# Seven block products instead of eight in rounds of the second channel layer, where attention stands still

## The chip, the cores and the metric

The kernel runs on one core of a Trainium2 chip. The metric is device time in microseconds (us) for one execution. A core has five engines with instruction queues of their own: TensorE (PE, matmuls; its weight loads are listed as PEld), VectorE (DVE), ScalarE (ACT), GpSimd (POOL) and SyncE (SP, which issues DMAs). A matmul writes to PSUM, from where DVE or ACT move or add the result to SBUF. Engines wait for one another through semaphores.

## The reference

Attention with a block mask is followed by a Fourier mixing block. Cut to what matters:

```python
# q, k, v: (4 batches, 8 heads, 768 tokens, 64), float32
scores = scale * np.matmul(q, k.transpose(0, 1, 3, 2))      # masked by blocks of 32
attn = softmax(scores)                                      # written out in full
x = heads_side_by_side(np.matmul(attn, v))                  # (4, 768, 512)

X = np.fft.fft(np.fft.fft(x, axis=1), axis=2)
u = x + np.real(X)
un = (u - mean(u)) / np.sqrt(var(u) + 1e-06)
ch = np.maximum(un @ w_ch1, 0.0) @ w_ch2                    # 512 -> 2048 -> 512
return u + ch
```

The last line but one holds the two channel layers. The change is in the second, `... @ w_ch2`.

## The kernel before, in words

**Order of the work.** The program is written out in full by a Python planner. Attention runs over 4 batches x 4 pairs of heads, in slots: a slot has the scores (L577, `s`), the exponential (L597), the mask multiply (L607) and the products with the values (L651, `o`); sums of the weights are made by POOL (L637). The Fourier and channel work of a batch is done while attention works on later batches. For that it is put into two lists: `apart`, small steps of the Fourier part (transforms `zp`, `pq`, statistics, whitening `un`, transposes `utp`, sums for the next products), and `late`, the channel steps. A model of the engines, `busy(engine, us)`, keeps a clock for PE, ACT, DVE and POOL, and `gap(...)` puts those steps of `apart` into the stream whose inputs and PSUM bank are free by that model. `until(met)` empties `late` until a condition holds. It is called where the attention of batch b needs the buffer x of batch b-2, and at the very end. While it runs, attention stands still: no new scores are issued.

**Halves.** The 768 tokens of a batch are folded into two halves of 384, with sums in xA and xB (tiles of 128 x 3 x 512). A half has three token groups m of 128.

**Rounds.** The 2048 hidden columns are done in rounds r = 0..3 of 512. A round begins with two quads (`quad(p)`), each of which makes two of the round's four hidden blocks of 128 for both halves, by a scheme with seven products for a 2 x 2 block product (L1066, tiles `xp`, `yp`, `z5`, `z7`), and leaves hA and hB after the relu. Then comes the second layer. In batches 0 to 2, `channels(r, half, m)` runs six times: four matmuls of 128x512 (`y`, L1122) into a PSUM tile of its pool, and one DVE sum `x += y` (L1125). In the records of the profile an fp32 matmul shows as two. In the last batch, `outputs(r, m, after)` does two rounds at once with seven block products of 128x256 (`yy`, L1187), whose PSUM tiles come from four different pools (`ps_m`, `ps_t`, `ps_s`, `ps_o`); its DVE sums are L1194 and L1217, an ACT copy L1204, and its left-hand sums L1170.

**Names that matter below.** `right` (L1028) makes the first layer's right-hand sums on DVE. L760 and L802 scale x and fold the Fourier parts, L886 to L903 are the matmuls of `pq`, L936 and L925 belong to statistics and `x += un`, L950 whitens, L991 transposes `un` (24 matmuls for a batch, `utp`), and L992 copies the result. `place` (L674, `xt`) writes the attention output into x. `store(half, m)` sends a finished token group to the output on SP's queue.

In the seven-product scheme, for blocks a of the hidden values (by half and by the first or second 256 of the round's hidden columns) and blocks B of the weights, sums of blocks are multiplied and the results are shared between output blocks, so that seven products of 128x256 do the work of eight.

Of the kernel before, what the change touches and what calls it, by code (L numbers as in the profile page):

```python
# [11 lines left out]
FP32 = mybir.dt.float32  # L12
# [5 lines left out]
ALU = mybir.AluOpType  # L18
ACT = mybir.ActivationFunctionType
# [80 lines left out]
def kernel(  # L100
# [14 lines left out]
    nc = tc.nc  # L115

    B, H, S, D = q.shape
    DM = H * D
    FF = w_ch1.shape[1]
    P = 128  # L120
# [56 lines left out]
    ep = ctx.enter_context(tc.tile_pool(name="ep", bufs=4))  # L177
    acc_p = ctx.enter_context(tc.tile_pool(name="acc_p", bufs=2))
    sum_p = ctx.enter_context(tc.tile_pool(name="sum_p", bufs=1))
    big = ctx.enter_context(tc.tile_pool(name="big", bufs=1))  # L180
    tr_p = ctx.enter_context(tc.tile_pool(name="tr_p", bufs=2))
    zc_p = ctx.enter_context(tc.tile_pool(name="zc_p", bufs=1))
# [12 lines left out]
    def busy(engine, us, after=0.0):  # L195
        when[engine] = max(when[engine], after) + us
        return when[engine]

    def bank(tag):

        at = free[tag].index(min(free[tag]))
        when["PE"] = max(when["PE"], free[tag][at])
        free[tag][at] = float("inf")
        return tag, at
# [6 lines left out]
    def room(i, shape, name, dtype=FP32):  # L211
        return big.tile(shape, dtype, tag=f"big{i}", name=name)
# [764 lines left out]
    def mixer(b, xA, xB):  # L977
# [75 lines left out]
        def quad(p):  # L1053

            g = p // 2 % 2 if last else 0
            if p % 2 == 0:
                for i in range(2):
                    hs[g, i] = room((2, 0)[g] + i, [P, 4, HS], "h" + "AB"[i])
            l1, l2 = 2 * (p % 2), 2 * (p % 2) + 1
            h11, h12, h21, h22 = (hs[g, i][:, l, :] for l in (l1, l2) for i in range(2))  # L1060
            a11, a12, s2, a22 = blocks(p)
            b11, b21, b22 = unT[0][:, K1, :], unT[0][:, K2, :], unT[1][:, K2, :]

            def product(to, a, c, after=0.0):
                for k in range(ND // 2):
                    nc.tensor.matmul(to, a[:, k, :], c[:, k, :], start=(k == 0),  # L1066
                                     stop=(k == ND // 2 - 1))
                return busy("PE", PRODUCT, after) + HOP

            def plus(to, ps, a, at):  # L1070
                tt(out=to, in0=ps, in1=a, op=ALU.add)  # L1071
                return busy("DVE", SUM, at) + HOP

            def relu(h, at):
                nc.scalar.activation(out=h, in_=h, func=ACT.Relu)  # L1075
                busy("ACT", RELU, at)

            def combine(j):
                left(p + 1, j)
                busy("DVE", COMBINE)  # L1080

            x, at = ps_m.tile([P, 512], FP32, tag="m", name="xp")[:, 0:HS], bank("m")
            z5, z7 = (ps_s.tile([P, 2, 512], FP32, tag="s", name=name)[:, 0, 0:HS]
                      for name in ("z5", "z7"))
            done = product(x, a11, b11)
            nc.scalar.copy(out=h11, in_=x)  # L1086
            p1 = busy("ACT", RELU, done) + HOP
            give(at, p1 - HOP)
            y, at = ps_m.tile([P, 512], FP32, tag="m", name="yp")[:, 0:HS], bank("m")
            p2 = product(y, a12, b21)  # L1090
            done = product(z7, s2, t[2])
            u2 = plus(h21, z7, h11, max(done, p1))
            c11 = plus(h11, y, h11, p2)
            relu(h11, c11)
            done = product(z5, s[1], t[1])
            plus(h12, z5, h21, done)
            combine(1)
            done = product(z7, s[3], t[3], u2)
            u3 = plus(h21, z7, h21, done)
            c22 = plus(h22, z5, h21, done)  # L1100
            z_at[0] = c22
            relu(h22, c22)
            combine(3)
            gap(0.0, 1.9)
            done = product(y, a22, t[4], c11)
            c21 = plus(h21, y, h21, done)
            give(at, c21 - HOP)
            relu(h21, c21)
            gap(0.0, 1.9, "t")
            done = product(z7, s[4], b22, u3)  # L1110
            z_at[1] = plus(h12, z7, h12, done)
            relu(h12, z_at[1])
            combine(4)
            if last:
                for j in ((1, 2), (3, 4))[p % 2]:
                    output_right(p // 4, j, p // 2 % 2)

        def channels(r, half, m):

            y, at = ps_m.tile([P, DM], FP32, tag="m", name="y"), bank("m")  # L1120
            for l in range(4):
                nc.tensor.matmul(y, hs[0, half][:, l, m * P:(m + 1) * P], w2_sb[:, 4 * r + l, :],  # L1122
                                 start=(l == 0), stop=(l == 3))
            x = (xA, xB)[half]
            nc.vector.tensor_tensor(out=x[:, m, :], in0=y, in1=x[:, m, :], op=ALU.add)  # L1125
            give(at, busy("DVE", 0.7, busy("PE", 3.45) + HOP))
            if r == NF // 4 - 1:
                store(half, m)

        def store(half, m, cols=slice(0, DM), queue=nc.sync):  # L1130
            x = (xA, xB)[half]
            for p0, cnt, rows in _rows(out[b][:, cols], T * half + m):
                queue.dma_start(out=rows, in_=x[p0:p0 + cnt, m, cols])
            if m == out_of[half][-1]:
                finished.add((b, half))

        last = b == B - 1  # L1140
        OUT = (2, 0, 1)
        out_of = (OUT, OUT if last else (0, 1, 2))
# [131 lines left out]
    short, apart, late, due = deque(), deque(), deque(), deque()  # L1274
    asked = set()
    needed = set()
    state = {"paired": False, "total": None, "w": 0, "got": 0, "owed": 0.0, "ready": 0.0}

    def channel_step():
        late.popleft()[0]()  # L1280
# [6 lines left out]
    def do_apart():  # L1287
        kind, fn, pe, act, dve, _ = apart.popleft()
        if kind[0] in "dw":
            dve += behind(kind)  # L1290
            state["ready"] = busy("DVE", dve, rstd_at[0] if kind == "w" else state["ready"]) + HOP
            fn()
            return
        done = state["ready"]
        if kind != "-":
            at = bank(kind[0])
            done = busy("PE", pe, done) + HOP
        fn()
        if act:
            done = busy("ACT", act, done) + HOP  # L1300
        if dve:
            done = busy("DVE", dve, done) + HOP
        if kind != "-":
            give(at, done - HOP)
        state["ready"] = done

    def gap(rest=0.0, ahead=None, kinds="tm"):

        used = "".join(k for k in "tm" if k not in kinds)
        if ahead is None:  # L1310
            ahead = AHEAD if late else ALONE
        while apart:
            kind, fn, pe, act, dve, need = apart[0]
            if len(late) > need:
                break
            if kind[0] in "dw":
                dve += behind(kind)
                if kind == "w" and rstd_at[0] > max(when["DVE"], when["PE"]) + 0.2:
                    break
                if max(when["DVE"], state["ready"]) + dve > when["PE"] + rest + ahead:  # L1320
                    break
            elif kind != "-":
                bank_at = max(min(free[k]) for k in kind)
                if (any(k in used for k in kind) or
                        max(state["ready"], bank_at) > when["PE"] + 0.1):
                    break
                used += kind
            do_apart()
        for item in list(short):
            kind, ready, fn = item  # L1330
            if kind not in used and max(ready, min(free[kind])) <= when["PE"] + 0.1:
                used += kind
                short.remove(item)
                fn()

    def until(met):

        while not met():
            if late:
                channel_step()  # L1340
                gap(2.0)
            else:
                do_apart()

    def begin(b):

# [16 lines left out]
    def once(*of):  # L1363
        if of in asked:
            return False
        asked.add(of)
        return True
# [11 lines left out]
    def slot(sl):  # L1379
# [46 lines left out]
        if s == 0 and 0 < n < len(pairs) - 1:  # L1426
            load_k(n + 1)

        reuse = n % NP == 0 and phase >= 2
        if s >= (5 if reuse else 3) and (n, 0) in oT_at and once(n):  # L1430
            b, j = pairs[n]
            at = oT_at[n, 0]
            if reuse:
                until(lambda: (b - 2, 0) in finished)
                at = when["PE"] + LEAVES
            if in_blocks(n):
                place_blocks(n, 0)
            else:
                short.append(("t", at, lambda: place(n, 0)))
# [97 lines left out]
        if sl == B * SB - 2:  # L1537
            over = nc.values_load(flag[0:1, 0:1], min_val=0, max_val=1)
    begin(B - 1)
    until(lambda: len(finished) == 2 * B)  # L1540
    ordered.close()


# [102 lines left out]
```

## Time and profile before

| What | Value |
|---|---|
| Median of 3 runs | 1062.39 us (1061.66 to 1063.84) |
| The profiled execution's own time | 1061.69 us |
| Span of that execution (first to last instruction) | 1060.0 us |
| Mean granted TensorE clock | 0.994 |
| DVE, ACT, POOL busy | 669.1, 366.5, 240.5 us |
| Matmuls of L1122 (`y`) | 576 records, 256.1 us busy |
| Matmuls of L1187 (`yy`), in the page's chain of waits | 7% of the span |
| Matmuls of L1122 in the chain of waits | 23% of the span |
| HBM traffic | 36.72 MB read, 6.29 MB written |

Durations in the page's groups are those of single instructions; for PE they overlap, so that the time a stream of matmuls takes is read from the starts of successive rows in the order in time. The last column of a group's row is the idle time of the engine just before its instructions, with the engine, tile and line that ended it. In a table by windows, the numbers after the window are its length and, for PE, PEld, DVE, ACT and POOL in turn, the busy time and count; then the granted clock (PEclk, 1.00 is full speed), the DMA share and GB/s. Rows of the order in time are: start, length, engine, line, operation, output and inputs, partitions and shape, count, and in brackets the idle time before and what ended it.

### The profile page before, as it was taken

The page shows a single profiled execution, that of the slowest core. Times are in us where ns is not written, and L with a number is a line of the kernel's source. Part 1 is how long each engine was busy: PE and PEld are TensorE (multiplying, and loading weights), DVE is VectorE, ACT ScalarE, POOL GpSimd, SP SyncE. Part 2 cuts the span into 40 slices and gives each one's busy share as a digit, 9 for nine tenths or more (in the row PEclk, how much of TensorE's full clock was granted, in tenths as well). Part 3 has the DMA queues.
Part 4 walks back from the last instruction along what each step waited for, and adds up shares of the span by engine and source line. Part 5 has one row for each costly group of instructions (what it writes and reads, how often), then busy time and mean ns, then how long its engine had stood idle before and what let it go on. Part 6 is the DMA issues. An engine that isn't in the chain of part 4 may idle for free.

```text
span 1060.0 us, 12495 instructions
## 1 busy us (share of the span) xinstructions
PE 1030.6 (97%) x4414; PEld 537.1 (51%) x4414; DVE 669.1 (63%) x1227; ACT 366.5 (35%) x736; POOL 240.5 (23%) x270
## 2 busy tenths in 40 slices
PE   8989999999999999999999999899999999999996
PEld 4333345445465454443534654354445564578585
DVE  6898795877746345655678364765447446774663
ACT  6978755564020122433441212343221111210210
POOL 1000183556000002554552001635420001000000
PEclk9999999999999999999999999999999999999998
DMA  7757522220000002231220001210000001000001
GB/s 217 229 166 222 112 46 45 45 46 15 1 1 0 1 1 57 52 56 27 41 54 0 1 1 44 63 33 19 8 15 0 1 0 42 19 1 1 0 18 46
DMA packets 120544, 46.27 MB, mean 44 GB/s; under 512 B 108172, under 2 KB 113562, under 8 KB 120474
## 3 DMA queue, kind: packets, MB, share of 16 engines
q1 hardware_dynamic: 119222, 44.66, 17.6%
q10 hardware_dynamic: 1220, 0.72, 0.3%
q8 instruction: 36, 0.59, 0.2%
q14 instruction: 34, 0.28, 0.1%
q0 software_dynamic: 32, 0.01, 0.0%
HBM read 36.72 MB, written 6.29 MB: 41 GB/s over the span
## 4 chain that ended last, share of the span: by engine, by line
PE 87%; DVE 6%; ACT 4%; issue 2%; DMA 1%; SPq 0%; POOL 0%; ACTq 0%; DVEq 0%; POOLq 0%
PE y L1122 23%; PE z L1066 16%; PE s L577 11%; PE o L651 10%; PE yp L1066 8%; PE yy L1187 7%; PE xp L1066 4%; PE zp L855 2%; PE s L587 1%; DVE t L1028 1%; ACT e L597 1%; PE sp L718 1%; PE sp L732 1%; PE utp L991 1%; PE xt L674 1%
## 5 line engine op out<-in xcount | busy, mean ns | idle before, releaser
L637 POOL TENSOR_TENSOR acc<-acc,e 128x384 f32<-128x384 f32 x158 | 160.9, 1052 | 87.1 <-DVE e L607 68.0
L577 PE MATMUL s<-qT,kT 64*128 64x384 f32 x768 | 154.8, 518 | 7.4 <-ACT e L597 5.8
L651 PE MATMUL o<-e,vr 128*64 128x384 f32 x768 | 143.1, 500 | 2.2 <-DVE oT L659 2.2
L1125 DVE TENSOR_TENSOR x<-y,x 128x512 f32<-128x512 f32 x72 | 49.8, 691 | 130.1 <-PE y L1122 129.8
L1122 PE MATMUL y<-w_sb,hB 128*128 128x512 f32 x288 | 128.0, 595 | 0.3 <-DVE x L1125 0.3
L1122 PE MATMUL y<-w_sb,hA 128*128 128x512 f32 x288 | 128.1, 594 | 0.0
L607 DVE TENSOR_TENSOR e<-s,mask 128x768 f32<-128x768 f32 x88 | 80.0, 950 | 48.9 <-ACT s L605 39.9
L577 PEld LDWEIGHTS s<-qT,kT 64*128 64x128 f32 x768 | 64.5, 187 | 85.7 <-ACT e L597 23.6
L605 ACT ACTIVATE s<-s 128x768 f32<-128x768 f32 x88 | 66.7, 792 | 92.6 <-PE s L577 92.4
L637 POOL TENSOR_TENSOR acc<-e 128x384 f32<-128x384 f32 x46 | 50.3, 1113 | 212.0 <-ACT e L597 125.9
L597 ACT ACTIVATE e<-s 128x768 f32<-128x768 f32 x104 | 79.1, 810 | 49.0 <-PE s L587 36.4
L1066 PE MATMUL z<-unT,t 128*128 128x384 f32 x256 | 93.4, 487 | 0.6 <-DVE hA L1071 0.6
L1122 PEld LDWEIGHTS y<-w_sb,hB 128*128 128x128 f32 x288 | 53.5, 190 | 65.5 <-issue 64.6
L1122 PEld LDWEIGHTS y<-w_sb,hA 128*128 128x128 f32 x288 | 53.6, 190 | 62.6 <-issue 59.9
L651 PEld LDWEIGHTS o<-e,vr 128*64 128x64 f32 x768 | 48.0, 136 | 72.7 <-issue 67.8
L1071 DVE TENSOR_TENSOR hA<-z,hA 128x384 f32<-128x384 f32 x64 | 35.7, 557 | 70.6 <-PE z L1066 70.6
L1075 ACT ACTIVATE hA<-hA 128x384 f32<-128x384 f32 x64 | 33.6, 524 | 122.5 <-DVE hA L1071 122.4
L1066 PEld LDWEIGHTS z<-unT,t 128*128 128x128 f32 x256 | 48.2, 190 | 35.6 <-DVE hA L1071 3.0
L1075 ACT ACTIVATE hB<-hB 128x384 f32<-128x384 f32 x64 | 33.6, 525 | 86.0 <-DVE hB L1071 86.0
L938 POOL TENSOR_SCALAR st<-st 128x1 f32<-128x1 f32 x24 | 8.3, 347 | 207.4 <-DVE st L937 207.3
L1086 ACT COPY hA<-xp 128x384 f32<-128x384 f32 x32 | 15.3, 479 | 111.6 <-PE xp L1066 111.6
L1066 PE MATMUL z<-t,w_sb 128*128 128x384 f32 x128 | 46.7, 488 | 0.7 <-DVE t L1028 0.7
(207 smaller groups left out, 1430.7 us busy)
## 6 DMA issues: line engine op xcount, KB each, us to landing
wraw<-in_moe_w_ch_dram SPq DMA_DIRECT2D x32, 512.0 KB
vr<-in_v_dram SPq DMA_DIRECT2D x30, 192.0 KB
qb<-in_q_dram SPq DMA_DIRECT2D x44, 96.0 KB
kb<-in_k_dram SPq DMA_DIRECT2D x44, 96.0 KB
x<-oT SPq DMA_DIRECT2D x192, 12.0 KB
out_dram<-x SPq DMA_DIRECT2D x11, 252.0 KB
out_dram<-x SPq DMA_DIRECT2D x18, 128.0 KB
qr<-in_q_dram SPq DMA_DIRECT2D x24, 64.0 KB
```

The lines of the kernel that those rows point to most:

```text
L577: nc.tensor.matmul(s[:, i, 0:HS], kT[rows, c * P:(c + 1) * P], qT[rows, queries], start=True, stop=u not in by_pe)
L597: nc.scalar.activation(out=e, in_=s[:, :, 0:HS], func=ACT.Exp, scale=scale)
L605: nc.scalar.activation(out=s[:, :, 0:HS], in_=s[:, :, 0:HS], func=ACT.Exp, scale=scale)
L607: nc.vector.tensor_tensor(out=e, in0=s[:, :, 0:HS], in1=m.broadcast_to([P, 2, HS]), op=ALU.mult)
L637: nc.gpsimd.tensor_add(out=acc[:, i, :], in0=start[:, i, :], in1=e[:, i, :])
L651: nc.tensor.matmul(o[D * i:D * i + D, :], vt[:, i, c, :], e[:, i, :], start=(c == 0), stop=(c == C - 1))
L1066: nc.tensor.matmul(to, a[:, k, :], c[:, k, :], start=(k == 0), stop=(k == ND // 2 - 1))
L1071: tt(out=to, in0=ps, in1=a, op=ALU.add)
L1075: nc.scalar.activation(out=h, in_=h, func=ACT.Relu)
L1122: nc.tensor.matmul(y, hs[0, half][:, l, m * P:(m + 1) * P], w2_sb[:, 4 * r + l, :], start=(l == 0), stop=(l == 3))
L1125: nc.vector.tensor_tensor(out=x[:, m, :], in0=y, in1=x[:, m, :], op=ALU.add)
L1187: nc.tensor.matmul(ps, a[:, k, :], c[k // 2][:, k % 2, :] if isinstance(c, list) else c[:, k, :], start=(k == 0), stop=(k == 3))
```

## The change

In batches 0 to 2, the quad that begins a round while `until(..., alone=True)` runs marks that round as one of seven products. That holds for eight of the twelve rounds: all four of batch 0, and the last two (r = 2, 3) of batches 1 and 2. In the second quad of such a round, outstanding sums of attention are drained, four buffers of the mask tiles' pool `ep` are taken as room, and POOL makes four right-hand sums of weight blocks (`round_right`). Then `round_of(r, m)` replaces the six `channels` steps by three, one for each token group, both halves together. Each has seven products of two matmuls of 128x256, all into the four quarters of one PSUM tile `ps` (two banks, pool `ps_s` with two buffers). The results are taken up by three ACT copies (`keep`), DVE sums straight from PSUM (`plus`, and one over both halves), and three POOL sums of what was kept (`later`). The left-hand sums of the next group are made by DVE (1, 2) and POOL (3, 4). Stretches of attention stand still one slot earlier than before where `late` is not empty (s = 4 instead of 5). The two halves of a batch now finish together. The core of the diff:

```diff
+            if not last:
+                if p % 2 == 0:
+                    seven[p // 2] = state["alone"]
+                elif seven[p // 2]:
+                    state["drain"]()
+                    sums_room()
+                    for j in (1, 2, 4, 3):
+                        round_right(p // 2, j)
...
+        def sums_room():
...
+            rooms = [ep.tile([P, 2 * HS], FP32, tag="e", name="of") for _ in range(4)]
+            w_t[1] = wt_p.tile([P, 2, DH], FP32, tag="wt", name="wt")
...
+        def round_right(r, j):
+            a, c = {1: (part(r, 0, 1), part(r, 0, 0)), 2: (part(r, 1, 1), w_t[1]),
+                    3: (part(r, 1, 1), part(r, 0, 1)), 4: (part(r, 1, 0), w_t[2])}[j]
+            nc.gpsimd.tensor_tensor(out=w_t[j], in0=a, in1=c, op=ALU.subtract)
+            busy("POOL", 1.35)
...
+        def round_left(m, j):
+            a11, a12, a21, a22 = tokens(m)
+            to, a, c, op = {1: (h_s[1], a21, a22, ALU.add), 2: (a21, h_s[1], a11, ALU.subtract),
+                            3: (h_s[3], a22, a21, ALU.subtract),
+                            4: (h_s[4], a12, a21, ALU.subtract)}[j]
...
+        def round_of(r, m):
...
+            ps = ps_s.tile([P, 2, 512], FP32, tag="s", name="yz")
+            u_at, c_at, d_at, o_at = ps[:, 0, 0:DH], ps[:, 0, DH:DM], ps[:, 1, 0:DH], ps[:, 1, DH:DM]
+
+            def product(to, a, c, start):
+                for k in range(2):
+                    nc.tensor.matmul(to, a[:, k, :], c[:, k, :], start=start and k == 0,
+                                     stop=k == 1, skip_group_check=True)
+                return busy("PE", 0.87) + HOP
...
+            done = product(u_at, a11, part(r, 0, 0), True)
+            k0 = keep(0, u_at, done)
+            done = product(c_at, a12, part(r, 1, 0), False)
+            k0 = max(k0, plus(a0, c_at, done))
+            later(a0, 0, k0)
+            gap(0.0, 1.9)
+            done = product(o_at, a22, w_t[4], True)
+            plus(b0, o_at, done)
+            if m == OUT[0]:
+                round_left(m, 3)
+                round_left(m, 4)
+            done = product(u_at, a21, w_t[2], False)
+            k1 = keep(1, u_at, done)
+            later(a1, 1, k1)
+            done = product(d_at, h_s[1], w_t[1], False)
+            k2 = keep(2, d_at, done)
+            ahead(1, 2)
+            gap(0.0, 1.9)
+            done = product(u_at, h_s[3], w_t[3], False)
+            tt(out=both, in0=both, in1=_at(ps[:, 0, :], 0, [(0, 2), (1, DH)]), op=ALU.add)
+            at = busy("DVE", 0.7, done) + HOP
+            later(b1, 2, max(at, k2))
+            ahead(3)
+            done = product(d_at, h_s[4], part(r, 1, 1), False)
+            plus(a1, d_at, done)
+            ahead(4)
+            gap(0.0, 1.9)
+            z_at[0] = z_at[1] = when["DVE"]
...
         def channels(r, half, m):
 
+            if seven.get(r):
+                round_of(r, m)
+                if m == OUT[-1]:
+                    for _ in range(T):
+                        late.popleft()
+                return
...
-    def until(met):
+    def until(met, alone=False):
+
+        state["alone"] = alone
...
+        def drain():
+            while due:
+                sum_up()
+        state["drain"] = drain
+
-        if s >= (5 if reuse else 3) and (n, 0) in oT_at and once(n):
+        if s >= ((4 if late else 5) if reuse else 3) and (n, 0) in oT_at and once(n):
...
-                until(lambda: (b - 2, 0) in finished)
+                until(lambda: (b - 2, 0) in finished, s == 4)
...
+    state["drain"] = lambda: None
+    until(lambda: len(finished) == 2 * B, True)
```

In the changed kernel's trace the seven products' matmuls stand on L1181.

More of the change, by code (lines that the diff above doesn't have):

```diff
@@ L179 @@
     sum_p = ctx.enter_context(tc.tile_pool(name="sum_p", bufs=1))
+    wt_p = ctx.enter_context(tc.tile_pool(name="wt_p", bufs=1))
     big = ctx.enter_context(tc.tile_pool(name="big", bufs=1))
@@ L1116, in quad, with cut @@
                     output_right(p // 4, j, p // 2 % 2)
-        def channels(r, half, m):
+        seven = {}
+        w_t, h_s, kept = {}, {}, {}
+        def sums_room():
+            def cut(t, at, k):
+                return t[:, at:at + 2 * HS // 3 * k].rearrange("p (k n) -> p k n", k=k)
+            rooms = [ep.tile([P, 2 * HS], FP32, tag="e", name="of") for _ in range(4)]
+            w_t[1] = wt_p.tile([P, 2, DH], FP32, tag="wt", name="wt")
+            for t, j in zip(rooms, (2, 3, 4)):
+                w_t[j] = t[:, 0:2 * DH].rearrange("p (k n) -> p k n", n=DH)
+            for t, j in zip(rooms, (1, 3, 4)):
+                h_s[j] = t[:, 2 * DH:2 * HS].rearrange("p (k n) -> p k n", n=P)
+            for i in range(3):
+                kept[i] = rooms[3][:, i * DH:(i + 1) * DH]
@@ new lines, in part, with tokens @@
+        def part(r, k, n):
+            return w2_sb[:, 4 * r + 2 * k:4 * r + 2 * k + 2, n * DH:n * DH + DH]
+        def round_right(r, j):
[3 more added lines that the diff above has]
+            busy("POOL", 1.35)
+        def tokens(m):
+            return [hs[0, i][:, 2 * k:2 * k + 2, m * P:(m + 1) * P]
+                    for i in range(2) for k in range(2)]
@@ new lines, in round_left @@
+        def round_left(m, j):
[3 more added lines that the diff above has]
+                            4: (h_s[4], a12, a21, ALU.subtract)}[j]
+            if j > 2:
+                nc.gpsimd.tensor_tensor(out=to, in0=a, in1=c, op=op)
+                busy("POOL", 0.75, when["DVE"])
+            else:
+                tt(out=to, in0=a, in1=c, op=op)
+                busy("DVE", 0.43)
@@ new lines, in round_of, with keep, plus, later @@
+        def round_of(r, m):
+            after = dict(zip(OUT, OUT[1:])).get(m)
+            a11, a12, a21, a22 = tokens(m)
+            a0, a1 = xA[:, m, 0:DH], xA[:, m, DH:DM]
+            b0, b1 = xB[:, m, 0:DH], xB[:, m, DH:DM]
+            both = xB[:, m, :].rearrange("p (n d) -> p n d", n=2)
+            ps = ps_s.tile([P, 2, 512], FP32, tag="s", name="yz")
[5 more added lines that the diff above has]
+                return busy("PE", 0.87) + HOP
+            def keep(i, src, done):
+                nc.scalar.copy(out=kept[i], in_=src)
+                return busy("ACT", 0.36, done) + HOP
+            def plus(to, src, done):
+                tt(out=to, in0=src, in1=to, op=ALU.add)
+                return busy("DVE", 0.43, done) + HOP
+            def later(to, i, at):
+                nc.gpsimd.tensor_add(out=to, in0=kept[i], in1=to)
+                busy("POOL", 0.75, at)
+            def ahead(*js):
+                if after is not None:
+                    for j in js:
+                        round_left(after, j)
+            if m == OUT[0]:
+                round_left(m, 1)
+                round_left(m, 2)
+            done = product(u_at, a11, part(r, 0, 0), True)
[6 more added lines that the diff above has]
+            plus(b0, o_at, done)
+            if m == OUT[0]:
+                round_left(m, 3)
[17 more added lines that the diff above has]
+            z_at[0] = z_at[1] = when["DVE"]
+            if r == NF // 4 - 1:
+                store(0, m)
+                store(1, m)
@@ L1133, in store @@
                 queue.dma_start(out=rows, in_=x[p0:p0 + cnt, m, cols])
-            if m == out_of[half][-1]:
+            if cols.stop == DM:
+                stored[half] += 1
+            if stored[half] == T:
                 finished.add((b, half))
+        stored = [0, 0]
         last = b == B - 1
@@ L1276 @@
     needed = set()
-    state = {"paired": False, "total": None, "w": 0, "got": 0, "owed": 0.0, "ready": 0.0}
+    state = {"paired": False, "total": None, "w": 0, "got": 0, "owed": 0.0, "ready": 0.0,
+             "alone": False, "drain": lambda: None}
     def channel_step():
@@ L1343, in until @@
                 do_apart()
+        state["alone"] = False
     def begin(b):
@@ L1539 @@
     begin(B - 1)
-    until(lambda: len(finished) == 2 * B)
+    state["drain"] = lambda: None
+    until(lambda: len(finished) == 2 * B, True)
     ordered.close()
```

## The prediction

> **What bounds the kernel.** I read the busy line and the chain first, then the groups by line and shape, then the order in time of the engines around the rounds.
>
> ```profile
> PE 1030.6 (97%) x4414; PEld 537.1 (51%) x4414; DVE 669.1 (63%) x1227; ACT 366.5 (35%) x736; POOL 240.5 (23%) x270
> PE 87%; DVE 6%; ACT 4%; issue 2%; DMA 1%; SPq 0%; POOL 0%; ACTq 0%; DVEq 0%; POOLq 0%
> ```
>
> TensorE is busy for 97% of the span and holds 87% of the chain. A PE microsecond taken out counts, and so does any hole put between two matmuls. DVE (63%), ACT and POOL have room on average; the question is where their results are awaited. The groups that give prices:
>
> ```profile
> L1122 PE MATMUL y<-w_sb,hA 128*128 128x512 f32 x288 | 128.1, 594 | 0.0
> L1125 DVE TENSOR_TENSOR x<-y,x 128x512 f32<-128x512 f32 x72 | 49.8, 691 | 130.1 <-PE y L1122 129.8
> L1187 PE MATMUL yy<-w_sb,hA 128*128 128x256 f32 x96 | 21.9, 381 | 0.0
> L1194 DVE TENSOR_TENSOR x<-yy,x 128x256 f32<-128x256 f32 x36 | 14.7, 422 | 14.9 <-PE yy L1187 14.2
> L1217 DVE TENSOR_TENSOR x<-x,u 128x512 f32<-128x512 f32 x6 | 4.2, 693 | 0.2
> L1204 ACT COPY u<-yy 128x256 f32<-128x256 f32 x6 | 2.2, 373 | 48.6 <-PE yy L1187 48.6
> ```
>
> Recorded matmul durations overlap, so the price of a matmul is the spacing of starts, from the order in time of PE:
>
> ```profile
> 266.76 10.46 PE L1122 MATMUL y<-w_sb,hA 128*128 128x512 f32 x24
> 277.06 10.46 PE L1122 MATMUL y<-w_sb,hB 128*128 128x512 f32 x24
> 287.36 1.45 PE L1066 MATMUL xp<-unT,w_sb 128*128 128x384 f32 x4
> ...
> 402.69 2.31 PE L1122 MATMUL y<-w_sb,hA 128*128 128x512 f32 x5
> 404.84 0.60 PE L991 MATMUL utp<-ident,un 128*128 128x128 f32 x4
> 405.79 3.70 PE L1122 MATMUL y<-w_sb,hB 128*128 128x512 f32 x8 [0.35 <-DVE x L1125]
> ...
> 953.03 3.66 PE L1187 MATMUL yy<-w_sb,hA 128*128 128x256 f32 x16
> ...
> 965.16 3.02 PE L1187 MATMUL yy<-w_sb,hA 128*128 128x256 f32 x13
> ```
>
> Today's round takes 287.36 - 266.76 = 20.60 us for 48 records without a hole. The last batch, which has seven products already, puts 56 records of 128x256 into 965.16 - 953.03 = 12.13 us: 0.2166 us each, without a hole either. There each product has a PSUM tile of its own.
>
> **The saving.** A round in seven products has 3 token groups of 7 products of 4 records: 84 x 0.2166 = 18.19 us, 2.41 less than 20.60. Eight of the twelve rounds change (four in batch 0, the last two of batches 1 and 2): -19.3 us.
>
> **The waits.** The seven products of a token group write to the quarters of one tile `ps` of two banks. The waits of the built program tell what follows: in all 24 groups, every product after the first waits for the reader of the product just before it (keep 0, the a0 sum, the b0 sum, keep 1, keep 2, the sum over both halves), whatever quarter that reader reads. Only the first product of a group goes freely, since its tile is the other buffer. So product and reader take turns, six times a group. `product` books 0.87 us on PE and no wait, so no work was ordered to stand there.
>
> What one turn costs is in the trace, since y's tile was also awaited once. The DVE row at that place:
>
> ```profile
> 405.04 0.69 DVE L1125 TENSOR_TENSOR x<-y,x 128x512 f32<-128x512 f32 x1 [1.93 <-PE y L1122]
> ```
>
> The last y record ends at 402.69 + 2.31 = 405.00, 0.16 after the next instruction of PE started (404.84); DVE starts 0.04 later; it ends at 405.73, and PE starts at 405.79, 0.06 later. Its eight records then take 3.70 us, where eight in an unbroken stream take 3.60 (884.44 in the same view): 0.10 for the exposed weight load. A turn is thus 0.16 + 0.04 + 0.06 + 0.10 = 0.36 us and the reader. The readers are three copies of 0.373 (L1204), two sums of 0.424 (L1194) and one of 0.69 (L1217): 2.66. Per group 6 x 0.36 + 2.66 = 4.82 us beside 6.06 us of products, in 24 groups +115.7 us. A round becomes some 33 us. Bounds: without the 0.10 for the load the turn is 0.26 and the sum 101 us; with 0.45, because two semaphores are awaited at two of the six places, it is 129.
>
> The quad shows the same kind of wait covered: its z7 tile is read between two products, but the z5 product (1.29 us) stands there, and the 256 z records of that group have 0.6 us of waits on DVE's hA in all. A covering product is what the new order lacks.
>
> The Trainium skill (Perfetto Trace Analysis, Matmuls) asks that independent matmul groups rotate through different PSUM banks, so that the evacuation of one overlaps the next. The two sets of rows agree: the last batch does so and has no hole. By this page the change is built the wrong way round, and the sum is unchanged.
>
> **What lies in the waits.** At two of the six places the planner may put other PE steps. In the built order 12 stand at such a place: seven of some 0.9 to 1.7 us (parts of the Fourier steps), which cover a whole wait of about 0.75, and five groups of four transposes of 0.45: 7 x 0.75 + 5 x 0.45 = -7.5 us. From 5 to 12.
>
> **Side costs.** Four of the rounds begin with DVE scalings (L760 882 ns, L802 about 660, L925 463) queued ahead of the first left sums; the a0 sum stands behind them and the third product behind it. Counted off the DVE order, less what the first two products cover: 1.0 + 1.0 + 2.1 + 0.7 = +4.8 us. At the end of batch 2 all 24 transposes `utp` now follow the last round, where before channel rounds lay between them; the tail of it is already bare today:
>
> ```profile
> 900.81 0.66 PE L991 MATMUL utp<-ident,un 128*128 128x128 f32 x4 [0.27 <-DVE un L950]
> 902.13 0.66 PE L991 MATMUL utp<-ident,un 128*128 128x128 f32 x4 [0.66 <-DVE un L950]
> ```
>
> The DVE rows from the last `pq` to the first quad (sums, statistics, whitening, left and right sums) add to 12.75 us with 2.6 of PE beside them: 10.2 idle where the trace has 3.2 now, +7.0. Where attention resumes after batches 0 and 1, the transposes of x and the mask multiplies stand behind DVE and ACT work that used to lie beside rounds: +3.8. POOL's eight right sums (`round_right`), and a quad kept waiting behind them: +1.3. Within a group the other new work lies beside the 11 us: POOL five sums (two left, three `later`) of an estimated 0.7, two thirds of L637's 1052 ns for 128x384, 3.5 us; DVE 2.0 of readers and two left sums of 0.42. Nothing; if POOL ran late, the sixth product, which takes a POOL sum, would wait for it. The stores are the same transfers in another order, at the round's end: nothing, or with their cover gone one of them, under 1. DVE sums with SBUF operands only were seen to grow from 0.42 to 1.22 us (L1028) beside a POOL sum; the readers above read PSUM, and were not.
>
> **The clock.** Windows of the trace, with PE's busy time first and PEclk:
>
> ```profile
> 66.85:70.27 3.42, 0.88 (x10) 0.23 (x4) 2.17 (x9) 2.18 (x4) 0.00 (x0) 1.00 0.84 321
> 70.27:73.69 3.42, 3.42 (x14) 1.39 (x13) 3.28 (x7) 3.42 (x8) 0.00 (x0) 0.50 0.95 310
> 681.25:684.67 3.42, 1.25 (x8) 0.46 (x8) 3.42 (x6) 1.59 (x2) 2.24 (x2) 1.00 0.00 0
> 684.67:688.09 3.42, 3.42 (x12) 1.17 (x12) 2.92 (x3) 0.00 (x0) 2.65 (x3) 0.50 0.10 14
> 899.00:904.00 5.00, 2.67 (x19) 1.77 (x18) 4.11 (x9) 2.35 (x4) 2.03 (x4) 1.00 0.45 94
> ```
>
> A stretch with PE busy for 26% or 37% was followed by 3.4 us at half clock; 53% was not. The changed rounds hold 6.06 / (6.06 + 4.82) = 56%: I take full clock there, and one fall (+1.9) at batch 2's end.
>
> The Trainium skill (TensorE: Matmul & The Clock Gate, What's actually happening) has the clock fall after an idle window of about 3.4 us. By that rule the rounds, never idle for 1.2 us, keep the full clock; the rows show falls at windows that were only mostly idle, so I leave room.
>
> **The sum**, on the profiled execution's 1061.69 us (span 1060.0 and 1.69 around it, 0.70 under the median): -19.3 + 115.7 - 7.5 + 4.8 + 7.0 + 3.8 + 1.3 + 1.9 = +107.7, so 1169.4, and on the median 1170.
>
> **Rivals.** (1) *The waits cost nothing and the kernel is faster*: readers finish while PE still drains, as in the last batch, and the starting and resuming costs are covered as well. Left are -19.3 and the end of batch 2 (8.9): 1052. It decides if a turn exposes under 19.3 / 144 = 0.13 us even with no side cost. Against it: the waits are in the program, and the measured turn is 0.36 without its reader. (2) *The waits cost nothing, the side costs stay* (18.8): 1062, no change. (3) *Only readers of the same bank hold a product up*: products alternate banks but for the first two, so one wait of 0.36 + 0.373 per group stays exposed, the others lie behind a product of 0.866: 24 x 0.73 = 17.6, and with the side costs 1062.39 - 19.3 + 17.6 + 18.8 = 1079.5. The program's waits speak against it too.
>
> The Trainium skill (PSUM — Partial Sum Buffer, PSUM bank collisions raise a hardware error) asks for guards by bank and quadrant, not by whole tile; by that rule alone rival 3 would be the result, but the program waits for more.
>
> (4) *The clock halves in the rounds.* If the gate's limit lies above 56%, windows alternate: slow ones double the products' spacing, and their share of busy time rises to 72%, which restores the clock. Half of the 6.06 us doubled in 24 groups is +73: 1243.
>
> **Chances.** Forecast 0.82, (1) 0.03, (2) 0.03, (3) 0.04, (4) 0.08. The low end takes the turn at 0.26, 11 us covered and half the side costs: 1062.4 - 19.3 + 101 - 11 + 9 = 1142. The high end takes 0.45, 5 covered, side costs of 28 and a quarter of rival 4: 1062.4 - 19.3 + 129 - 5 + 28 + 18 = 1213. That leaves out under 2 in 10. A measurement here can tell about 0.2% (2.1 us) from no change: faster 0.03, same 0.03, slower 0.94.
>
> **What would show it.** Right: L1181's `yz` has idle time of some 100 us ahead of it, released about half each by ACT's keeps and DVE's sums; PE's share falls to about 88%; a round lasts some 33 us with PEclk at 9; rows of 0.22 spacing inside a product. Wrong: `yz` back to back with idle under 0.2 per product (rivals 1, 2), one hole per group (3), or PEclk of 5 in batch 0's rounds (4). The prediction falls as a whole if the waits seen in the program are met before PE arrives.

## The result and the profile after

The changed kernel takes 1182.26 us (median of 4 runs, 1175.73 to 1186.09) against 1062.03 before: 1.1124 times as long (95% interval 1.1065 to 1.1184). The profiled execution is the shortest of the four, 1175.73 us, with a span of 1174.0. The forecast was 1169.4 for the profiled execution and 1170 for the median.

The busy line and the chain of the changed kernel's page:

```profile
PE 1049.2 (89%) x4702; PEld 582.8 (50%) x4702; DVE 713.4 (61%) x1323; ACT 392.5 (33%) x808; POOL 368.4 (31%) x422
PE 27%; issue 6%; DVE 4%; POOL 2%; ACT 1%; SPq 1%; DMA 0%; POOLq 0%; DVEq 0%; ACTq 0%
```

PE's share fell from 97% to 89%; the other engines have no more of a share than before, POOL excepted. The chain names only 41% of the span here, so nothing is read from it. The groups by line and shape say where PE waited:

```profile
L1181 PE MATMUL yz<-of,hB 128*128 128x256 f32 x192 | 54.6, 407 | 27.9 <-DVE x L1190 27.6
L1181 PE MATMUL yz<-w_sb,hA 128*128 128x256 f32 x192 | 51.8, 392 | 13.1 <-ACT of L1186 13.1
L1186 ACT COPY of<-yz 128x256 f32<-128x256 f32 x72 | 26.7, 371 | 187.5 <-PE yz L1181 142.5 <-POOL of L1163 42.5 <-DVE x L928 2.5
L1190 DVE TENSOR_TENSOR x<-yz,x 128x256 f32<-128x256 f32 x72 | 30.5, 424 | 76.6 <-PE yz L1181 76.5
L1224 DVE TENSOR_TENSOR x<-x,yz 128x512 f32<-128x512 f32 x24 | 16.5, 686 | 43.5 <-PE yz L1181 39.9 <-issue 3.4
```

The readers cost what they cost in the last batch before (371, 424 and 686 ns, where it was 373, 422 and 693), and they wait for `yz`, while `yz` waits for them. Over the five groups of `yz` (two are shown) the idle time ahead is 27.9 + 13.1 + 11.8 + 23.1 + 10.9 = 86.8 us: 50.7 of it ended by DVE's sums and 34.6 by ACT's copies, where the prediction had looked for some 100, half each. The turns cost more than that idle time, since the four records of a product behind a wait span 1.10 to 1.13 us, all counted as busy, where products in a stream start 0.866 apart. One steady token group, in the order in time of PE:

```profile
278.52 1.03 PE L1181 MATMUL yz<-w_sb,hA 128*128 128x256 f32 x4
280.07 1.13 PE L1181 MATMUL yz<-w_sb,hA 128*128 128x256 f32 x4 [0.52 <-ACT of L1186]
281.78 1.13 PE L1181 MATMUL yz<-of,hB 128*128 128x256 f32 x4 [0.59 <-DVE x L1190]
283.43 1.13 PE L1181 MATMUL yz<-of,hB 128*128 128x256 f32 x4 [0.52 <-DVE x L1190]
285.07 1.13 PE L1181 MATMUL yz<-wt,of 128*128 128x256 f32 x4 [0.51 <-ACT of L1186]
286.81 1.10 PE L1181 MATMUL yz<-of 128*128 128x256 f32 x4 [0.61 <-ACT of L1186]
288.85 1.10 PE L1181 MATMUL yz<-w_sb,of 128*128 128x256 f32 x4 [0.94 <-DVE x L1224]
289.79 1.03 PE L1181 MATMUL yz<-w_sb,hA 128*128 128x256 f32 x4
```

Six of seven products wait, for exactly the readers the prediction named, and the first product of the next group (289.79), whose tile is the other buffer, does not. From start to start: 1.55, 1.71, 1.65, 1.64, 1.74, 2.04 and 0.94; less 0.866 each, the six turns take 0.68, 0.84, 0.78, 0.77, 0.87 and 1.17. A group takes 11.27 us for 6.06 us of products, a round 33.8.

### The profile page after: what moved, and what is told of

Its sections match the earlier page's. It is cut to its first block, busy times and chain, and to the rows that moved or that the text cites. A ratio compares the mean times of both kernels' runs of the same rounds, so it can differ in the third digit from the quotient of the medians.

```text
span 1174.0 us, 13621 instructions
## 1 busy us (share of the span) xinstructions
PE 1049.2 (89%) x4702; PEld 582.8 (50%) x4702; DVE 713.4 (61%) x1323; ACT 392.5 (33%) x808; POOL 368.4 (31%) x422
## 5 line engine op out<-in xcount | busy, mean ns | idle before, releaser
L1194 POOL TENSOR_TENSOR x<-of,x 128x256 f32<-128x256 f32 x72 | 52.2, 726 | 260.4 <-DVE x L1190 141.5
L1186 ACT COPY of<-yz 128x256 f32<-128x256 f32 x72 | 26.7, 371 | 187.5 <-PE yz L1181 142.5
L652 PEld LDWEIGHTS o<-e,vr 128*64 128x64 f32 x768 | 47.7, 136 | 71.1 <-issue 68.9
L1181 PE MATMUL yz<-of,hB 128*128 128x256 f32 x192 | 54.6, 407 | 27.9 <-DVE x L1190 27.6
L1190 DVE TENSOR_TENSOR x<-yz,x 128x256 f32<-128x256 f32 x72 | 30.5, 424 | 76.6 <-PE yz L1181 76.5
L1181 PE MATMUL yz<-w_sb,hA 128*128 128x256 f32 x192 | 51.8, 392 | 13.1 <-ACT of L1186 13.1
L1181 PEld LDWEIGHTS yz<-of,hB 128*128 128x128 f32 x192 | 32.9, 191 | 47.9 <-DVE x L1190 36.7
L1075 PE MATMUL xp<-unT,w_sb 128*128 128x384 f32 x128 | 48.3, 500 | 0.0
L1181 PEld LDWEIGHTS yz<-w_sb,hA 128*128 128x128 f32 x192 | 34.2, 189 | 27.5 <-ACT of L1186 22.8
```

What stands on the lines that cost most here:

```text
L652: nc.tensor.matmul(o[D * i:D * i + D, :], vt[:, i, c, :], e[:, i, :], start=(c == 0), stop=(c == C - 1))
L1181: nc.tensor.matmul(to, a[:, k, :], c[:, k, :], start=start and k == 0, stop=k == 1, skip_group_check=True)
L1190: tt(out=to, in0=src, in1=to, op=ALU.add)
L1194: nc.gpsimd.tensor_add(out=to, in0=kept[i], in1=to)
```

## The experiments

The main theory: the loss is turns, made by seven products in one PSUM tile. Rivals: short products are slow in any tile; POOL is too slow; the earlier standstill or the stretches' ends carry it; the clock does.

**Four tiles instead of one.**

```diff
-            ps = ps_s.tile([P, 2, 512], FP32, tag="s", name="yz")
-            u_at, c_at, d_at, o_at = ps[:, 0, 0:DH], ps[:, 0, DH:DM], ps[:, 1, 0:DH], ps[:, 1, DH:DM]
+            ps, ps_d = (ps_s.tile([P, 2, 512], FP32, tag="s", name=name) for name in ("yz", "yd"))
+            u_at, d_at = ps[:, 0, 0:DH], ps_d[:, 0, 0:DH]
...
+            c_at, at = ps_m.tile([P, 512], FP32, tag="m", name="yc")[:, 0:DH], bank("m")
...
+            o_at, at = ps_m.tile([P, 512], FP32, tag="m", name="yo")[:, 0:DH], bank("m")
```

> The changed kernel, but u, d, c and o each get a PSUM tile (u and d from ps_s, c and o from ps_m); products, readers and their order are the same. Theory (turns): each of the six turns of a group cost 5.18 us over its 6.06 us of products in the changed kernel's trace, and they come from products waiting for readers of the shared tile only. All six go; what is left is the sum over both halves holding the next group's first product by 0.1 to 0.2. 1175.7 - 24 x 5.18 + 7.5 (Fourier steps that lay in the waits take their own time again) + 24 x 0.15 = 1062, between 1053 and 1072. Rival A (short products cost a handover whatever the tile, or DVE and ACT are late themselves): over 1140. Rival B (POOL's sums are too slow once the turns are gone): 1075 to 1110, with idle time of yz released by POOL.

Measured: 1072.44 us (1.0096 of before, 1.008 to 1.0111). 110 of the 120 us are gone with the tiles alone (c and o now come from another pool, and the planner books its banks); the same products, readers and sums remain. Rival A is out. A steady group in the order in time of PE, and the one hole of the round's first group:

```profile
271.09 1.10 PE L1181 MATMUL yz<-of,hB 128*128 128x256 f32 x4 [1.08 <-DVE hB L1166]
...
278.01 1.03 PE L1181 MATMUL yz<-of,hB 128*128 128x256 f32 x4
278.87 1.03 PE L1181 MATMUL yd<-wt,of 128*128 128x256 f32 x4
279.73 1.03 PE L1181 MATMUL yz<-of 128*128 128x256 f32 x4
```

Starts are 0.86 apart, as the prediction priced a product. The time stands 0.4 above the upper end expected; idle time of these products released by POOL was 0.5 us in all, so rival B isn't the cause.

**Two tiles of one bank each.**

```diff
-            ps = ps_s.tile([P, 2, 512], FP32, tag="s", name="yz")
-            u_at, c_at, d_at, o_at = ps[:, 0, 0:DH], ps[:, 0, DH:DM], ps[:, 1, 0:DH], ps[:, 1, DH:DM]
+            ps, ps_d = (ps_s.tile([P, 2, 512], FP32, tag="s", name=name) for name in ("yz", "yd"))
+            u_at, c_at, d_at, o_at = ps[:, 0, 0:DH], ps[:, 0, DH:DM], ps_d[:, 0, 0:DH], ps_d[:, 0, DH:DM]
```

> The changed kernel with two tiles of one bank each in place of one tile of two banks: u and c share one, d and o the other. Theory (turns): only the second product follows a product of its own tile at once, so one turn of 0.36 + 0.37 (0.68 in the changed trace) per group stays, 24 x 0.68 = 16 us over the kernel with four tiles: 1078, between 1070 and 1088. Rival A: over 1140. A rival by which the waits on a tile are all or nothing: like the changed kernel or like the one with four tiles, within 5 us.

Measured: 1088.87 us (1.026, 1.0244 to 1.0276): 16.4 over the kernel with four tiles, where 24 x 0.68 = 16.3 was worked out. The level is 0.9 above the range expected, since the kernel with four tiles had come out 10 above its own forecast. The order in time of PE has the one turn:

```profile
274.38 1.13 PE L1181 MATMUL yz<-w_sb,hA 128*128 128x256 f32 x4 [0.25 <-DVE x L1224]
276.03 1.13 PE L1181 MATMUL yz<-w_sb,hA 128*128 128x256 f32 x4 [0.52 <-ACT of L1186]
277.00 1.03 PE L1181 MATMUL yd<-of,hB 128*128 128x256 f32 x4
```

The second product, which follows one in its own tile at once, waits 0.52; the third doesn't. (The 0.25 at the first is the next group's tile waiting for the sum over both halves; it also stands in the kernel with four tiles, as 0.43 at 275.31.) From the third product on, the products alternate between two banks here as they do in the changed kernel. There, with both banks in one tile, they wait all the same; here, with a tile for each bank, they don't. So it is the tile that is awaited, not the bank. One turn, six turns: the loss follows their number. One wait a group is what the prediction's rival 3 had, at 17.6 us.

**The last batch of the kernel before, with one tile.** All else is as before.

```diff
+            tile = ps_s.tile([P, 2, 512], FP32, tag="s", name="yy")
+            cuts = iter([(0, 0), (0, 1), (1, 0), (1, 1)] * 2)
+
             def product(pool, tag, a, c):
-                ps = pool.tile([P, 512], FP32, tag=tag, name="yy")[:, 0:DH]
+                i, n = next(cuts)
+                ps = tile[:, i, n * DH:n * DH + DH]
```

> The kernel before, with only the last batch altered: the seven products of each of its six groups go into the quarters of one tile (ps_s) instead of tiles of four pools. Theory (a turn is 0.36 and the reader, whatever the product's length): products here last 1.73 us; readers are 0.42 five times and twice 0.42 once, so 6 x 0.36 + 2.96 = 5.1 us a group, and 0.06 more per turn as the changed kernel's trace showed it: 6 x 5.5 = 33, so 1094, between 1088 and 1100. Rival A (the turns are bad only because products of 0.87 us are short): under 1072.

Measured: 1094.71 us (1.0304, 1.0288 to 1.032), 32.1 over before, for 36 turns: 0.89 each.

```profile
965.35 1.99 PE L1191 MATMUL yy<-ot,hB 128*128 128x256 f32 x8 [0.52 <-DVE x L1198]
967.86 1.99 PE L1191 MATMUL yy<-ot,hB 128*128 128x256 f32 x8 [0.52 <-DVE u L1198]
```

The same 0.52 stands ahead of products twice as long, in a batch that the change doesn't touch. So the price goes with the tile and its reader, and not with the length of the product.

**The earlier standstill alone.** `seven[p // 2]` is set to `False`: every round has eight products, and the rest of the change stays.

> The changed kernel with every round of the first three batches left at eight products: what stays is that attention stands still one slot earlier, the order of the stretch, and the finish of both halves together. Theory (the turns carry nearly all): 1062 to 1066. Rival (the earlier standstill is a cost of its own): 1068 or more.

Measured: 1059.13 us (0.9977, 0.9967 to 0.9986), 2.5 under before. Neither the theory nor the rival expected a gain. This part of the change is a small gain by itself, and the fastest kernel of the study. Its profiled execution has no fall of the clock but at its end, where before had two more; whether that is the whole gain, and why the earlier place brings it, wasn't taken apart.

**Where the remaining 11 to 13 us go.** With four tiles, PE has 19.3 us less to do (by the prediction's price) than with the earlier standstill alone, yet the kernel takes 13.3 us more. First, u alone in `ps_s`, so that the next group's u is in the other buffer:

```diff
-            ps, ps_d = (ps_s.tile([P, 2, 512], FP32, tag="s", name=name) for name in ("yz", "yd"))
-            u_at, d_at = ps[:, 0, 0:DH], ps_d[:, 0, 0:DH]
+            ps = ps_s.tile([P, 2, 512], FP32, tag="s", name="yz")
+            u_at = ps[:, 0, 0:DH]
...
+            c_at, at = ps_t.tile([P, 512], FP32, tag="t", name="yc")[:, 0:DH], bank("t")
...
+            d_at, at = ps_m.tile([P, 512], FP32, tag="m", name="yd")[:, 0:DH], bank("m")
```

> The kernel with four tiles, with u alone in ps_s (so that u of the next group has the other buffer), c in ps_t, o and d in ps_m. Theory (turns): in the kernel with four tiles the next group's first product still waited for the sum over both halves, 5.5 us of PE idle and some 0.1 more for the exposed load in each of up to 16 groups. 1072.4 - 5.5 - 1.6 = 1065, between 1061 and 1069. Rival (DVE itself is full in these rounds, so the wait only moves on): 1070 or more.

Measured: 1070.37 us (1.0076, 1.0059 to 1.0094), 2.1 less (3.1, each against its own runs of before), not 7. The wait of `yz<-w_sb,hA` went from 5.5 to 0.0, but the transposes `utp` grew idle by 4.2, from 8.3 to 12.5 us, and the idle time ahead of all of PE's groups stayed, 39.6 and 40.5 us: the hole moved on, as the rival had it. That DVE is full, as the rival had it too, isn't shown. The transposes' group with u in two buffers:

```profile
L992 PE MATMUL utp<-ident,un 128*128 128x128 f32 x96 | 16.8, 307 | 12.5 <-DVE un L951 6.8 <-DVE sums L701 2.7 <-ACT unT L993 2.4
```

Then batch 2 goes back to eight products in this kernel, by `seven[p // 2] = state["alone"] and b < 2`, and after that only its last round, by `... and not (b == 2 and p == 6)`:

> Own tiles with u in two buffers, and batch 2's two rounds left at eight products. Theory: the forecast's terms for batch 2 (2 x 2.41 saved; first groups 2.75, bare transposes 7.0 and one clock fall 1.9 lost) make it a loss of 6.9 when the turns are gone, so this is 7 under the kernel with seven products in batch 2 too: near 1058, between 1054 and 1061. Rival (the savings hold and the tail is no worse than before): 5 over it.

> As the kernel with u in two buffers, but only the last round of batch 2 is left at eight products. Theory: the transposes at the end of batch 2 get their cover of y matmuls back, 7.0 + 1.9 less lost for 2.4 saved: 6 under the kernel with it, near 1059, between 1055 and 1063. Rival (the loss comes from the first groups, not from the bare transposes): as with it, within 3.

Measured: 1064.35 us (1.0019, 1.0007 to 1.003) and 1064.93 us (1.0033, 1.0022 to 1.0044), so 6.0 and 5.4 less than with both rounds of batch 2 (1070.37). The sizes of the differences, 7 and 6, were right; the levels were expected 6 lower, since the kernel with u in two buffers had come out 5 higher. Nearly all of batch 2's loss is in its last round. The group of transposes in the kernel without it:

```profile
L992 PE MATMUL utp<-ident,un 128*128 128x128 f32 x96 | 16.3, 300 | 8.0 <-ACT unT L993 3.0 <-DVE sums L701 2.7 <-DVE un L951 2.3
```

Of the 12.5 us, 4.5 are gone, all of them waits for `un` (6.8 to 2.3).

The clock has a share in these levels that wasn't taken apart. The profiled run with u in two buffers (mean clock 0.989) has five windows of 3.4 us at half clock before the kernel's end: at 71.1, at 422.7 and three from 903.9 on. The one with the earlier standstill alone (0.997) has none. In the twelve runs without batch 2's rounds, 1061.78 us goes with a mean clock of 0.998, and 1066.72 with 0.991.

**Only rounds that end no stretch.** `... and b < 2 and p < 6` in the kernel with u in two buffers: seven products in three rounds of batch 0 and one of batch 1.

> Own tiles with u in two buffers, seven products only in the first three rounds of batch 0 and in round 2 of batch 1: no round that ends a stretch. Theory: the last rounds' gain of 2.4 was lost to the bare steps where attention resumes (in the kernel without batch 2's rounds 0.63, 1.68, 1.94 and 1.28 us after batch 0), so the rest is a gain: 4 x 2.41 less some 4.3 for the first groups and the quads, 5 under the kernel with the earlier standstill alone: 1055, between 1052 and 1059. Rival (first groups and quads eat the gain in each round): 1059 or more.

Measured: 1061.88 us (1.0002, 0.9992 to 1.0013), level with before and 2.7 over the earlier standstill alone (0.0025 of 1062). By its time the rival is right: there is no gain of the seven products left. The order in time has holes of 1.08 and 0.99 in the first groups of two rounds, 1.24 in the quad between, and 0.52 and 0.18 behind; here is the first:

```profile
267.45 1.89 DVE L761 TENSOR_TENSOR x<-x,r 128x512 f32<-128x512 f32 x3
...
270.27 1.10 PE L1181 MATMUL yz<-of,hB 128*128 128x256 f32 x4 [1.08 <-DVE hB L1166]
```

Three scalings lie on DVE ahead of the left sums. These holes make 4.0 of the 12.3 us lost (9.6 saved, and 2.7 over). Another 3.2 lie ahead of the transposes `utp` (5.9 us idle, against 2.7 with the earlier standstill alone), and the profiled run has one window at half clock (684.6) that the other lacks, worth at most 1.7. The rest, some 3 us, isn't settled.

**The clock.** The changed kernel again, unaltered:

> The changed kernel once more, unaltered, with a profile. Its four runs lay between 1175.73 us (mean clock 0.991) and 1186.09 (0.978). Theory: the difference is falls of the clock that hit windows of 3.4 us in which PE was busy for under some 45% (the first groups of rounds, the end of batch 2), at other places from run to run as the windows lie; with a clock of 0.991 it takes 1176, at 0.979 it takes 1185, and the falls stand behind such windows. Rival (the clock falls inside the steady groups, busy for 70% by the records): falls of 3.4 us spread over all eight rounds.

Measured: 1188.52 us with a mean clock of 0.978. In the run of 1175.73 the clock fell after the start of the rounds only at 913.6 (one window of 3.4 us, in batch 2's first round) and at batch 2's end, from 1009.2 on (three). Here it fell at these two places too, and four times more: at 270.9 and 329.0 for four windows each, in the first round and the second, and at 486.0 and 762.5 for one each, where attention resumes. The windows around the first fall of this run:

```profile
267.53:270.94 3.41, 1.65 (x7) 1.17 (x8) 2.71 (x6) 0.30 (x2) 0.58 (x1) 1.00 0.00 0
270.94:274.35 3.41, 2.89 (x7) 1.49 (x5) 0.42 (x1) 0.00 (x0) 1.51 (x3) 0.50 0.00 0
274.35:277.77 3.42, 2.40 (x6) 1.32 (x5) 0.60 (x2) 0.75 (x2) 0.72 (x1) 0.50 0.00 0
277.77:281.18 3.41, 2.47 (x5) 1.53 (x6) 0.94 (x2) 0.00 (x0) 0.60 (x1) 0.50 0.00 0
281.18:284.59 3.41, 3.21 (x8) 2.02 (x6) 1.31 (x2) 0.11 (x1) 1.53 (x3) 0.50 0.02 5
```

And two windows of the run of 1175.73, the one with the same hole and the one behind the fall at 913.6:

```profile
268.48:271.89 3.41, 1.86 (x8) 1.00 (x6) 2.09 (x6) 0.00 (x0) 1.31 (x2) 1.00 0.00 0
913.60:917.01 3.41, 2.95 (x7) 1.86 (x7) 0.00 (x0) 0.37 (x1) 0.92 (x2) 0.50 0.00 0
```

The window with the first group's hole (1.41 us of idle, PE busy for 48%) is followed by a fall. In the other run the windows lie 0.7 us later against the hole; the one that holds it is busy for 55%, and no fall follows. The clock then stays at half: three windows with PE busy for 85, 70 and 72% by the records are each followed by another at half, and full clock returns after the fourth, with 94%. The window at 913.6, with 86%, was the only one of its fall. So the theory is right that each fall stands behind a window in which PE was busy for less than half, though three of the six windows ahead of falls here were busy for 46 to 48%, above its 45%. The steady groups start no fall, but their turns can keep the clock down once it is down, which the theory didn't have. The difference of 12.8 us between the two runs goes with the clock: the first two rounds are 10.2 us longer, and 1.6 and 1.3 come behind the falls at 486.0 and 762.5. The time of the four earlier runs rises as their mean clock goes down (0.991, 0.984, 0.979, 0.978).

## Why the prediction was right

**The waits.** Right in kind and place; six a group, each named by its reader, and none at the seventh start. The term was 4.82 us a group and measured 5.2: the three copies' turns averaged 0.78 instead of 0.73, the two sums' 0.81 instead of 0.78, the sum over both halves 1.17 instead of 1.05. 24 x 0.38 is 9 us, the largest error of the sum. Besides its reader a turn cost 0.41 on average, not 0.36, within the bounds given (0.26 and 0.45). By the four tiles the waits are worth 110 us net; forecast were 115.7 less the covered 7.5.

**The saving.** 2.41 a round from a spacing of 0.2166: four tiles show products 0.86 apart, and with u in two buffers there is a group of 6.05 without a hole (274.06 to 280.11). Right.

**Side costs.** The first groups' extra idle ahead of the third product was 0.82, 0.73, 1.47 and 0.16 over a steady group's 0.59: 3.2, where 4.8 was forecast. The end of batch 2 was right within 1.4: 7.0 more idle time ahead of the transposes was forecast, and it went from 3.0 to 8.6 us; for the whole last round 7.0 + 1.9 - 2.4 = 6.5, and 5.4 was measured without turns. For the resuming of attention, 3.8 was forecast; the idle time ahead of `s`, `o` and `xt` over the whole kernel went from 10.7 to 14.2 us, 3.5 more. The quad behind POOL's right sums, at 1.3, isn't seen in the changed kernel: its `z` groups idle for 1.3 us in all, as before. A hole of 1.2 stands there only in the kernels with two or four tiles. The earlier standstill had no price but that of the resuming; alone it gains 2.5, a term that the sum lacks. So the reading that rounds with own tiles would come out level (rival 2, 1062) holds for 1072.44 only within 10 us.

**The clock.** The sum took one fall more than before. The profiled run had one at batch 2's end, of three windows, and one in a round; the other runs had lower clocks, and the 6.5 us between the profiled run and the median go with them. The step that failed is the claim that 56% keeps the clock. The average does, but a first group's window, busy for 38% in one run (910.19 to 913.60) and 48% in the other (267.53 to 270.94), doesn't, and behind it the turns can hold the clock down. The 53% that the prediction had read beside a full clock came from a window of 5 us; the clock's own window there (899.71 to 903.12) is busy for 58%. So a part of what rival 4 described is in the result, though not for its reason: 6.5 us in the median and 12.8 in the longest run, of the 73 it had.

**How near it came.** The profiled run is 6.3 us over its forecast. The waits alone would make 9, and the clock adds to it; the side costs that came out smaller (1.6 at the first groups, 1.4 at the transposes, 1.3 at the quad) and the gain of the earlier standstill (2.5) took a part of it back. That much is luck.

**The page on the clock.** The Trainium skill (TensorE: Matmul & The Clock Gate, What's actually happening) names an idle window of about 3.4 us as the cause of a fall and a busy one of that length as its end. Here a window with PE busy for 48%, and idle for 1.41 us at the longest, was enough for a fall; windows busy for 70 to 85% did not end it, and one of 86% and one of 94% did. The measurement decides.

**The page on banks.** The Trainium skill (Perfetto Trace Analysis, Matmuls) was right against this change: rotation through tiles in different banks took 110 of 120 us off. Banks alone were not enough, since the products of the changed kernel alternate between the two banks of their tile from the third on, and waited for 0.51 to 0.94 us all the same.

## What to carry to other kernels

Count a PSUM tile, not its quarter or bank, as what a product waits for in a program like this one: look in the built program at what the first matmul of each product awaits, and price each such turn by the reader and some 0.3 to 0.5 us more. A saving in PE time of 12% per round is lost by some three exposed turns among its 21 products (2.41 / 0.78). Before work is taken out of the bounding engine, ask what it covered. Here the longer round had covered DVE scalings (holes of 1.0 to 1.1 us in first groups) and transposes at a stretch's end (4.5 us of waits that are gone with eight products in batch 2's last round).

## What the runs showed of the hardware that was not expected

The half clock can outlast its cause: after one window with PE busy for 48% it stayed for 13.7 us, in which PE was busy for 70 to 94% of each window by its records. Over all traces here, laid on the clock's own windows, every window at half clock before the kernel's end that was busy for 85% or less was followed by another, and every one with 86% or more by full clock. Falls are less sharp: from 43% to 51% some windows were followed by a fall and some not (43% without one, in the kernel with the earlier standstill alone at 679.97; 51% with one, in the kernel with one tile in the last batch at 899.65).

DVE and POOL sums took longer side by side. In the kernel with rounds that end no stretch, two DVE sums of 128x256 with SBUF operands took 1.32 and 1.37 us (291.88 and 293.23) while POOL sums of 128x512 ran, and one of the same shape took 0.41 behind them (295.58); the prediction had seen as much. New is POOL's own time: of its four sums of 128x512 there, the first, beside DVE sums of 128x1536 and 128x765, took 2.79 us (286.84), the third 1.27.
